# Float64 weight tiles on the sync queue, nine steps ahead in three buffers, and later reciprocal products in the first three pairs of heads

## The chip, the cores and the metric

The kernel runs on one core of a Trainium2 chip. The metric is the device time of one execution in microseconds. Engines are named as in the profile: PE is the matrix engine (PEld its weight loads), DVE the vector engine, ACT the scalar engine, POOL GpSimd, SP the sync engine, which only issues transfers. An engine works through its own instructions in order, and so does the queue that it issues transfers from.

## The reference, cut to what matters

Block-sparse attention over 4 batches of 8 heads (768 rows, head size 64), then a dense two-layer network on the joined heads:

```python
scores = np.where(mask, scale * np.matmul(q, k.transpose(0, 1, 3, 2)), -1e9)
attn = np.exp(scores - scores.max(-1, keepdims=True))
attn = attn / (attn.sum(-1, keepdims=True) + 1e-09)
x = np.matmul(attn, v)                    # joined to [3072, 512]
h = x @ w_in                              # w_in [512, 2048], float64
g = np.where(h >= 1, h, np.where(h <= -1, 0, (h + 1) ** 2 / 4))
out = g @ w_out                           # w_out [2048, 512], float64
```

The two weight matrices arrive as float64. [...]

## The kernel before, in words

**Steps.** All work is put on one plan: `at(t, fn)` gives a piece of work a time in steps, and the list sorted by these times is the order in which the pieces are written down. The framework then arranges each engine's instructions by this order and by its own estimate of when each is ready, so neighbours may change places. One step is one 128-column chunk of scores for half a head (384 rows); a head has 12 steps, head i starts at step 12 i. The constants `P`, `PW` (the first eight heads, called wide) and others hold each piece's distance in steps.

**A head.** `load_qk` (L214) loads q and k, `hi` and `lo` split them, four kinds of moves (L221, L237, L238, on SP) place the parts in KA, QA, KB, QB. `max_mm` (L267, PE) and `max_red` (L272, DVE) find row maxima, which `max_row` (L283) writes into QA. Then per step `scores` (L303, L304, PE), `expo` (L308, ACT) and `values`. For the first five pairs of heads (`WHOLE`) `values` is one full-precision matmul (L333); later heads split the exponentials in two (L196 on ACT, L316 on DVE) and use two (L335, L336), and POOL adds up the sums (L323).

**Reciprocals.** At the end of a pair of heads, for each half `hf`, the denominators go out to DRAM (`r_in`, L377 on ACT's queue), back as a small tile (L378, SP), through `recip` (L372, DVE), out again (`r_out`, L382, SP) and back spread over partitions (L384, SP: den<-s). Then `x_mul` (L387, DVE) multiplies the half's result by them, `x_hi` (ACT) and `x_lo` (L395, DVE) split it into x, which the network reads. These three stand at distances `xm`, `xh`, `xl` from a common time.

**Conversions.** `convert` makes three pieces of work: `load` (L162) brings 128 x 512 float64 values (512 KB) into a tile `raw`; `bits` is one ACT instruction (L168, Abs) and four DVE instructions (L169, L170, L172, L174), of which L172 and L174 read raw again; `split` rounds the high part (L196, ACT) and subtracts for the low one (L180, POOL). Conversion n stands at time t; its load stands at t - P["cl"], its split at t + 1.705. There are 16 of w_in, at CONV + n CSTEP, during the eight heads of batch 0, and 16 of w_out, every 3 steps from step 98.98 on, during the first half of the network. The w_out parts are also stored to DRAM (`w_keep`, L448, SP) right after the split, and later halves load them from there (L441).

**The network.** `moe` runs eight halves (4 batches, 2 halves of 384 rows), the first from step 99.67, each over 16 chunks of the inner dimension, 3 steps a chunk: first layer L457 to L459, nonlinearity L463 to L478, second layer L485 to L487. They run beside the next batch's heads; the last two run after the attention.

**Queues.** Every transfer is issued on SP except the raw tiles (`Q_RAW`, POOL) and `r_in`'s first one (ACT).

Of the kernel before, what the change touches and what calls it, by code (L numbers as in the profile page):

```python
# [10 lines left out]
I32 = mybir.dt.int32  # L11
# [7 lines left out]
B, H, S, D = 4, 8, 768, 64  # L19
# [5 lines left out]
NP = H // 2  # L25
# [3 lines left out]
KA = 96 + T  # L29
# [8 lines left out]
def body(ctx, tc, qk_t, v, sampled_blocks, moe_w_in, moe_w_out, ind, cm, negd, ident, fold, out):  # L38
    nc = tc.nc
    pool = lambda name, bufs, **kw: ctx.enter_context(tc.tile_pool(name=name, bufs=bufs, **kw))  # L40
    cst = pool("cst", 1)
    ld = pool("ld", 1)
# [7 lines left out]
    mt = pool("mt", 2)  # L50
    op = pool("op", 1)
    wst = pool("wst", 3)
    cv = pool("cv", 1)
# [12 lines left out]
    Q_KEEP = nc.sync  # L66
    Q_W = nc.sync
    Q_OUT = nc.sync
    Q_RAW = nc.gpsimd
    Q_QK = nc.sync  # L70
    Q_V = nc.sync

    def f(ap):
        return ap.bitcast(F32)
# [12 lines left out]
    def consts():  # L87
        M = slice(64, KM)
        for i in range(SETS):
            nc.gpsimd.memset(f(QA[i][64:128 if i == 0 else 96]), 0.0)  # L90
        nc.gpsimd.memset(VW[0][:, :, 64:128], 1.0)
        nc.gpsimd.memset(VW[1][:, :, 0:64], 1.0)
        nc.vector.memset(eps, 1e-9)
        nc.vector.memset(half_c, 0.5)
        sraw = cst.tile([128, NR, 2], I32, name="sraw")
        nc.sync.dma_start(out=sraw[M], in_=sampled_blocks.bitcast(I32).rearrange("a (r w) -> a r w", w=2))
        cmt = cst.tile([128, 2 * NB], F32, name="cmt")
        nc.sync.dma_start(out=cmt[M], in_=cm)
        ef = f(cv.tile([128, 512, 2], I32, name="raw", bufs=2).rearrange("p c w -> p (c w)"))[64:KA, 0:S]
        nc.sync.dma_start(out=ef, in_=ind)  # L100
        idf = pp.tile([128, HALF], F32, name="pt")[:, 0:128]
        nc.sync.dma_start(out=idf, in_=ident)
        nc.vector.tensor_copy(out=idr, in_=idf)
        nc.vector.tensor_copy(out=KAt[0][64:KA], in_=ef)
        nc.sync.dma_start(out=nd, in_=negd.rearrange("a (t p) -> a t p", t=T))
        nc.sync.dma_start(out=sel, in_=fold)
        for i in range(1, SETS):
            rounded(nc.gpsimd, KAt[i][64:KA], ef)
        sf = cst.tile([128, NR], F32, name="sf")
        nc.vector.tensor_copy(out=sf[M], in_=sraw[M, :, 0])  # L110
        al = cst.tile([128, NB], F32, name="al")
        nc.vector.tensor_copy(out=al[M], in_=cmt[M, 0:NB])
        for r in range(NR):
            nc.vector.scalar_tensor_tensor(
                out=al[M], in0=cmt[M, NB:2 * NB], scalar=sf[M, r:r + 1], in1=al[M],
                op0=ALU.is_equal, op1=ALU.max)
        mb = cst.tile([128, NB], F32R, name="mb")
        nc.vector.tensor_scalar(out=mb[M], in0=al[M], scalar1=-1.0, scalar2=BIG, op0=ALU.add, op1=ALU.mult)
        for hf in range(2):
            cs = slice(hf * HALF, (hf + 1) * HALF)  # L120
            pm = psa.tile([128, 512], F32, name="pa")
            nc.tensor.matmul(out=pm[0:NB, 0:HALF], lhsT=mb[M], rhs=KAt[0][64:KM, cs], start=True, stop=True)
            for i in range(SETS):
                (nc.scalar.copy if i else nc.vector.tensor_copy)(out=QA[i][64:KM, cs], in_=pm[0:NB, 0:HALF])
# [4 lines left out]
    def at(t, fn, *args):  # L129
        plan.append((t, fn, args))  # L130
# [18 lines left out]
    def plan_conversions():  # L149
        last = 1e9  # L150
        for t, load, bits, split in sorted(conv, key=lambda x: -x[0]):
            last = t = min(t, last - P["cd"])
            at(t - P["cl"], load)
            at(t, bits)
            at(t + P["cs"], split)

    def convert(t, src, dst, done=None):
        st = {}

        def load():  # L160
            st["raw"] = cv.tile([128, 512, 2], I32, name="raw", bufs=2)
            Q_RAW.dma_start(out=st["raw"], in_=src.bitcast(I32).rearrange("p (c w) -> p c w", w=2))  # L162

        def bits():
            raw = st["raw"]
            lo32, hi32 = raw[:, :, 0], raw[:, :, 1]
            a = st["a"] = cv.tile([128, 512], I32, name="cva", bufs=2)
            nc.scalar.activation(out=f(a), in_=f(hi32), func=AF.Abs)  # L168
            nc.vector.tensor_scalar(out=f(a), in0=f(a), scalar1=CLO, scalar2=CHI, op0=ALU.max, op1=ALU.min)  # L169
            nc.vector.tensor_scalar(out=a, in0=a, scalar1=3, scalar2=0x3FFFFFFF,  # L170
                                    op0=ALU.logical_shift_left, op1=ALU.bitwise_and)
            nc.vector.scalar_tensor_tensor(out=a, in0=hi32, scalar=-0x40000000, in1=a,  # L172
                                           op0=ALU.bitwise_and, op1=ALU.bitwise_or)
            nc.vector.scalar_tensor_tensor(out=a, in0=lo32, scalar=29, in1=a,  # L174
                                           op0=ALU.logical_shift_right, op1=ALU.bitwise_or)

        def split():
            hi, lo = dst()
            rounded(CH, hi, f(st["a"]))
            nc.gpsimd.tensor_tensor(out=lo, in0=f(st["a"]), in1=f(hi), op=ALU.subtract)  # L180
            if done:
                done()

        conv.append((t, load, bits, split))
# [13 lines left out]
    def head(i, n0, b, h, pst):  # L198

        j, e = divmod(h, 2)  # L200
        wide = i < H
        whole = i // 2 in WHOLE
        G = {**P, **PW} if wide else {**P, **PA} if i < 2 * H else P
        o0, o1 = (L, R) if e == 0 else (R, L)
        QAi, KAi = QA[i % SETS], KAt[i % SETS]
        st = {}
# [191 lines left out]
        for hf in range(2):  # L398
            for c in range(T):
                at(s, scores, hf, c)  # L400
                at(s + G["ex"], expo, c)
                if not whole:
                    at(s + G["ph"], p_hi, c)
                    at(s + G["pl"], p_lo, c)
                    at(s + G["ps"], p_sum, hf, c)
                at(s + G["lag"], values, hf, c)
                s += 1
            u = s - 1 + G["lag"]
            if whole:
                at(u + G["ow"], o_whole, hf)  # L410
            else:
                at(u + G["ot"], o_tmp)
                at(u + G["oa"], o_add, hf)
                at(u + G["al"], acc_sum, hf)
                if e:
                    at(u + G["su"], sums, hf)
                    at(u + G["de"], dens, hf)
            if e:
                y = u + (G["yw"] if whole else G["yy"])
                if whole:  # L420
                    at(y, r_in, hf)
                    y += G["r1"]
                at(y, recip, hf)
                at(y + 0.1, r_out, hf)
                y -= G["r1"]
                y += G["r2"]
                at(y + G["xm"], x_mul, hf)
                at(y + G["xh"], x_hi, hf)
                at(y + G["xl"], x_lo, hf)
# [4 lines left out]
    def moe(t0, p, b, hf, first):  # L434

        g = {}
        G = {**P, **PM} if first else P

# [4 lines left out]
        def w_dst(fi):  # L443
            w = g["w", fi] = wst.tile([128, 2, DM], F32R, name="w")
            return w[:, 0], w[:, 1]
# [60 lines left out]
        for fi in range(NF):  # L506
            u = t0 + fi * p
            if first:
                convert(u + 1.5 * p - P["co"], moe_w_out[fi * 128:(fi + 1) * 128, :], lambda fi=fi: w_dst(fi),
                        lambda fi=fi: w_keep(fi))  # L510
# [16 lines left out]

    at(TC, consts)
    for i in range(NHEADS):
# [5 lines left out]
    p = PER * H / (2 * NF)  # L535
# [3 lines left out]
    for fq in range(4):  # L539
        for kt in range(4):  # L540
            cs = slice(fq * 512, (fq + 1) * 512)
# [10 lines left out]


WHOLE = (0, 1, 2, 3, 4)
P = {'vw': 4.0, 'r1': 0.857, 'r2': 4.031, 'qs': 9.647, 'ks': 11.666, 'vs': 9.131, 'ld': 5, 'm0': 7.832, 'm1': 5.0, 'mr': 0.46, 'mc': 2.3, 'mt': 1.325, 'mw': 0.9, 'ex': 0.524, 'ph': 1.22, 'pl': 1.349, 'ps': 0.841, 'ow': 0.704, 'ot': 0.2, 'oa': 0.549, 'ah': 0.3, 'al': 0.578, 'su': 0.637, 'de': 1.414, 'yw': 0.799, 'yy': 2.173, 'xm': 0.774, 'xh': 1.0, 'xl': 2.518, 'gr': 0.1, 'gs': 0.279, 'gm': 0.314, 'gh': 0.934, 'gl': 1.232, 'l2': 1.494, 'l3': 0.158, 'l1': 0.121, 'cl': 3.327, 'cs': 1.705, 'cd': 1.8, 'co': 5.196, 'lag': 3.5}
PW = {'vw': 4.0, 'r1': 3.302, 'r2': 4.413, 'qs': 12.454, 'vs': 9.131, 'ld': 5, 'm0': 7.8, 'm1': 5.61, 'mr': 0.15, 'mc': 2.3, 'mt': 1.3, 'mw': 0.9, 'ex': 0.2, 'ph': 1.231, 'pl': 1.349, 'ps': 0.841, 'ow': 0.722, 'ot': 0.2, 'oa': 0.462, 'ah': 0.3, 'al': 0.578, 'su': 0.637, 'de': 1.525, 'yw': 0.813, 'yy': 2.024, 'xm': 0.516, 'xh': 1.1600000000000001, 'xl': 2.268, 'lag': 3.403}
TC = -90
H0 = 0.711
PH1 = ()
PH2 = ()  # L560
# [10 lines left out]
NHEADS = B * H  # L571
NMOE = B
PER = 2 * T
CONV, CSTEP = 6.105, 5.609
CLO, CHI = (struct.unpack("<f", struct.pack("<I", w))[0] for w in (0x38100000, 0x47EFFFFF))

_INS = ["qk_t", "v", "sampled_blocks", "moe_w_in", "moe_w_out"]
# [49 lines left out]
```

## Time and profile before

| | us |
|---|---|
| median of 3 runs (lowest, highest) | 1031.86 (1029.77, 1033.98) |
| profiled execution, its own time | 1029.55 |
| span in the profile | 1027.5 |
| PE busy | 956.7 |
| DVE busy | 751.0 |
| ACT busy | 635.4 |
| POOL busy | 396.0 |

The span runs from the first to the last instruction; the profiled execution's own time is a little more. An engine's busy time is the time in which at least one of its instructions ran. In the views a line such as L162 is a line of the kernel, `raw<-in_moe_w_in_dram` is what it writes and reads, and in a view of waits "A <- B: us, times, longest" says that A stood idle until B was done.

### The profile page before, as it was taken

How to read it: one execution, taken by the hardware profiler on the slowest of the kernel's cores; microseconds unless marked ns; L12 is line 12 of the kernel's file. 1: busy time of each engine (PE TensorE's matmuls, PEld its weight loads, DVE VectorE, ACT ScalarE, POOL GpSimd, SP SyncE). 2: the span in 40 equal slices, each digit the busy share in tenths (PEclk: the TensorE clock that was granted, in tenths of full speed). 3: DMA queues.
4: the chain of work that ended last, by engine and by line, in shares of the span. 5: the costliest groups of instructions: out<-in, count | busy, mean ns of one | idle time of the engine just before them, and what ended most of it. 6: DMA issues, size and time to landing. Idle time of an engine off the chain costs nothing.

```text
span 1027.5 us, 14635 instructions
## 1 busy us (share of the span) xinstructions
PE 956.7 (93%) x4687; PEld 828.1 (81%) x4687; DVE 751.0 (73%) x1317; ACT 635.4 (62%) x1302; POOL 396.0 (39%) x347
## 2 busy tenths in 40 slices
PE   3889887998889999999999999999999999999998
PEld 2556565777778989888988888988988899899997
DVE  5877787768999787888888887888888786422222
ACT  3566565557657666766767676766667666533433
POOL 3424233236656445454545445453545444100000
PEclk9999899999999999999999999999999999999999
DMA  6656666746435555554535455554535452433433
GB/s 169 184 153 168 182 157 199 217 146 187 152 121 165 146 146 152 147 173 127 156 122 162 137 162 152 147 167 125 151 120 178 131 144 83 149 124 123 154 131 105
DMA packets 56216, 154.43 MB, mean 150 GB/s; under 512 B 9612, under 2 KB 17952, under 8 KB 56140
## 3 DMA queue, kind: packets, MB, share of 16 engines
q1 hardware_dynamic: 51492, 136.70, 44.9%
q0 software_dynamic: 4608, 16.78, 5.6%
q8 instruction: 37, 0.61, 0.2%
q14 instruction: 39, 0.32, 0.1%
q10 hardware_dynamic: 40, 0.03, 0.0%
HBM read 100.92 MB, written 14.81 MB: 113 GB/s over the span
## 4 chain that ended last, share of the span: by engine, by line
PE 60%; DVE 12%; ACT 2%; DMA 2%; issue 2%; SPq 0%; ACTq 0%
PE oa L485 7%; PE oa L487 7%; PE oa L486 7%; PE hp L457 6%; PE hp L459 6%; PE hp L458 6%; PE po L335 4%; PE pa L303 4%; PE pa L304 4%; PE po L336 4%; PE pa L267 3%; DVE mc L272 3%; DVE pl L316 3%; DMA qk<-in_qk_t_dram 2%; DVE gl L478 2%; DVE xun L387 2%
## 5 line engine op out<-in xcount | busy, mean ns | idle before, releaser
L323 POOL TENSOR_TENSOR acc<-acc,pt 128x384 f32<-128x384 f32 x176 | 198.3, 1127 | 202.4 <-ACT pt L308 184.5
L272 DVE TENSOR_REDUCE mc<-pa 128x1 f32<-128x384 f32 x384 | 202.8, 547 | 23.7 <-PE pa L267 20.9
L316 DVE TENSOR_TENSOR pl<-pt,ph 128x384 fp32r<-128x384 f32 x264 | 177.5, 672 | 36.7 <-ACT ph L196 35.8
L196 ACT CAST ph<-pt 128x384 fp32r<-128x384 f32 x264 | 135.6, 514 | 98.2 <-PE po L335 94.9
L308 ACT ACTIVATE pt<-pa 128x384 f32<-128x384 f32 x288 | 140.6, 489 | 57.3 <-PE pa L304 48.5
L267 PE MATMUL pa<-KA,QA 88*128 88x384 f32 x384 | 143.4, 390 | 28.1 <-DVE mc L272 18.5
L457 PE MATMUL hp<-x,wi 128*128 128x384 f32 x448 | 156.9, 350 | 5.3 <-DVE r L469 5.3
L485 PE MATMUL oa<-w,gh 128*128 128x512 f32 x384 | 153.6, 400 | 0.3 <-ACT gh L196 0.3
L458 PE MATMUL hp<-x,wi 128*128 128x384 f32 x448 | 152.2, 340 | 0.0
L459 PE MATMUL hp<-x,wi 128*128 128x384 f32 x448 | 151.6, 338 | 0.0
L487 PE MATMUL oa<-w,gl 128*128 128x512 f32 x384 | 151.5, 395 | 0.0
L486 PE MATMUL oa<-w,gh 128*128 128x512 f32 x384 | 150.9, 393 | 0.0
L478 DVE TENSOR_TENSOR gl<-r,gh 128x384 fp32r<-128x384 f32 x128 | 102.6, 802 | 30.6 <-ACT gh L196 28.7
L267 PEld LDWEIGHTS pa<-KA,QA 88*128 88x128 f32 x384 | 73.9, 194 | 59.9 <-DVE mc L272 35.1
L469 DVE SCALAR_TENSOR_TENSOR r<-r,hp 128x384 f32<-128x384 f32 x112 | 61.6, 550 | 74.8 <-ACT r L466 74.8
L228 POOL TENSOR_TENSOR qk<-qk,qkh 128x768 f32<-128x768 f32 x32 | 62.1, 1940 | 119.0 <-ACT qkh L196 110.3
L303 PE MATMUL pa<-QA,KA 102*128 102x384 f32 x288 | 100.8, 350 | 6.2 <-DVE mc L272 5.2
L304 PE MATMUL pa<-QB,KB 128*128 128x384 f32 x288 | 98.1, 341 | 0.0
L463 ACT ACTIVATE r<-hp,half_c 128x384 f32<-128x384 f32 x112 | 65.1, 581 | 52.8 <-PE hp L459 49.7
L335 PE MATMUL po<-ph,vn 128*128 128x384 f32 x264 | 92.0, 349 | 4.2 <-DVE xun L345 3.2
L457 PEld LDWEIGHTS hp<-x,wi 128*128 128x128 f32 x448 | 84.8, 189 | 12.3 <-DVE r L469 7.8
L336 PE MATMUL po<-pl,vn 128*128 128x384 f32 x264 | 88.8, 336 | 0.0
(99 smaller groups left out, 1720.7 us busy)
## 6 DMA issues: line engine op xcount, KB each, us to landing
w<-wo_dram SPq DMA_DIRECT2D x112, 512.0 KB
qk<-in_qk_t_dram SPq DMA_DIRECT2D x32, 384.0 KB
raw<-in_moe_w_in_dram POOLq DMA_DIRECT2D x16, 512.0 KB, 6.2
raw<-in_moe_w_out_dram POOLq DMA_DIRECT2D x16, 512.0 KB, 4.2
wo_dram<-w SPq DMA_DIRECT2D x16, 512.0 KB
lv<-in_v_dram SPq DMA_DIRECT2D x32, 192.0 KB
KA<-qkh SPq DMA_DIRECT2D x32, 192.0 KB
QA<-qkh SPq DMA_DIRECT2D x32, 192.0 KB
```

The source lines that it names most:

```text
L267: nc.tensor.matmul(out=pm[:, 0:HALF], lhsT=QAi[0:KM, t * 128:(t + 1) * 128], rhs=KAi[0:KM, kh * HALF:(kh + 1) * HALF], start=True, stop=True)
L272: nc.vector.reduce_max(out=st["mc"][:, t, kh:kh + 1], in_=st.pop(("pm", t, kh))[:, 0:HALF], axis=AX.X)
L303: nc.tensor.matmul(out=ps[:, 0:HALF], lhsT=KAi[0:KA, ks], rhs=QAi[0:KA, cs], start=True, stop=False)
L308: nc.scalar.activation(out=p, in_=st.pop(("ps", c))[:, 0:HALF], func=AF.Exp, scale=SCALE)
L316: (nc.gpsimd if i < 2 * H and c in PL1 else nc.vector).tensor_tensor(out=pl, in0=st["p", c], in1=f(st["ph", c]), op=ALU.subtract)
L323: nc.gpsimd.tensor_tensor(out=st["acc", hf], in0=prev, in1=st["p", c], op=ALU.add)
L457: nc.tensor.matmul(out=hv, lhsT=wi[:, j, 0, fs], rhs=x[:, 0], start=(j == 0), stop=False)
L458: nc.tensor.matmul(out=hv, lhsT=wi[:, j, 0, fs], rhs=x[:, 1], start=False, stop=False)
L459: nc.tensor.matmul(out=hv, lhsT=wi[:, j, 1, fs], rhs=x[:, 0], start=False, stop=(j == NP - 1))
L485: nc.tensor.matmul(out=o, lhsT=gh[:, ts], rhs=w[:, 0], start=(fi == 0), stop=False)
L486: nc.tensor.matmul(out=o, lhsT=gh[:, ts], rhs=w[:, 1], start=False, stop=False)
L487: nc.tensor.matmul(out=o, lhsT=gl[:, ts], rhs=w[:, 0], start=False, stop=(fi == NF - 1))
```

## The change

The raw tiles are loaded on SP's queue instead of POOL's. Their tile has three buffers instead of two (the constant `ef`, which is read once at the start, uses the same buffers). The load stands 9.0 steps before its conversion instead of 3.327. The w_in conversions stand at 8.0 + 5.75 n instead of 6.105 + 5.609 n; the w_out conversions stay where they were. For the first three pairs of heads, `x_mul`, `x_hi` and `x_lo` stand two steps later; the transfers before them do not move.

```diff
-    Q_RAW = nc.gpsimd
+    Q_RAW = nc.sync
...
-        ef = f(cv.tile([128, 512, 2], I32, name="raw", bufs=2).rearrange("p c w -> p (c w)"))[64:KA, 0:S]
+        ef = f(cv.tile([128, 512, 2], I32, name="raw", bufs=3).rearrange("p c w -> p (c w)"))[64:KA, 0:S]
...
-            st["raw"] = cv.tile([128, 512, 2], I32, name="raw", bufs=2)
+            st["raw"] = cv.tile([128, 512, 2], I32, name="raw", bufs=3)
...
-                y += G["r2"]
+                y += G["r2"] + (XLATE if wide and j < NP - 1 else 0)
...
-P = {..., 'cl': 3.327, ...}
+P = {..., 'cl': 9.0, ...}
...
+XLATE = 2.0
...
-CONV, CSTEP = 6.105, 5.609
+CONV, CSTEP = 8.0, 5.75
```

More of the change, by code (lines that the diff above doesn't have):

```diff
@@ L554 @@
 WHOLE = (0, 1, 2, 3, 4)
-P = {'vw': 4.0, 'r1': 0.857, 'r2': 4.031, 'qs': 9.647, 'ks': 11.666, 'vs': 9.131, 'ld': 5, 'm0': 7.832, 'm1': 5.0, 'mr': 0.46, 'mc': 2.3, 'mt': 1.325, 'mw': 0.9, 'ex': 0.524, 'ph': 1.22, 'pl': 1.349, 'ps': 0.841, 'ow': 0.704, 'ot': 0.2, 'oa': 0.549, 'ah': 0.3, 'al': 0.578, 'su': 0.637, 'de': 1.414, 'yw': 0.799, 'yy': 2.173, 'xm': 0.774, 'xh': 1.0, 'xl': 2.518, 'gr': 0.1, 'gs': 0.279, 'gm': 0.314, 'gh': 0.934, 'gl': 1.232, 'l2': 1.494, 'l3': 0.158, 'l1': 0.121, 'cl': 3.327, 'cs': 1.705, 'cd': 1.8, 'co': 5.196, 'lag': 3.5}
+P = {'vw': 4.0, 'r1': 0.857, 'r2': 4.031, 'qs': 9.647, 'ks': 11.666, 'vs': 9.131, 'ld': 5, 'm0': 7.832, 'm1': 5.0, 'mr': 0.46, 'mc': 2.3, 'mt': 1.325, 'mw': 0.9, 'ex': 0.524, 'ph': 1.22, 'pl': 1.349, 'ps': 0.841, 'ow': 0.704, 'ot': 0.2, 'oa': 0.549, 'ah': 0.3, 'al': 0.578, 'su': 0.637, 'de': 1.414, 'yw': 0.799, 'yy': 2.173, 'xm': 0.774, 'xh': 1.0, 'xl': 2.518, 'gr': 0.1, 'gs': 0.279, 'gm': 0.314, 'gh': 0.934, 'gl': 1.232, 'l2': 1.494, 'l3': 0.158, 'l1': 0.121, 'cl': 9.0, 'cs': 1.705, 'cd': 1.8, 'co': 5.196, 'lag': 3.5}
 PW = {'vw': 4.0, 'r1': 3.302, 'r2': 4.413, 'qs': 12.454, 'vs': 9.131, 'ld': 5, 'm0': 7.8, 'm1': 5.61, 'mr': 0.15, 'mc': 2.3, 'mt': 1.3, 'mw': 0.9, 'ex': 0.2, 'ph': 1.231, 'pl': 1.349, 'ps': 0.841, 'ow': 0.722, 'ot': 0.2, 'oa': 0.462, 'ah': 0.3, 'al': 0.578, 'su': 0.637, 'de': 1.525, 'yw': 0.813, 'yy': 2.024, 'xm': 0.516, 'xh': 1.1600000000000001, 'xl': 2.268, 'lag': 3.403}
 TC = -90
+XLATE = 2.0
 H0 = 0.711
```

## The prediction

> **What bounds the kernel now.** I read the page first, for the engines' shares; then busy time by stretches, cut where the exponentials show a head's beginning; then the waits of each engine inside the stretch that stands out; then the timeline of a few places in it. The page:
>
> ```profile
> span 1027.5 us, 14635 instructions
> PE 956.7 (93%) x4687; PEld 828.1 (81%) x4687; DVE 751.0 (73%) x1317; ACT 635.4 (62%) x1302; POOL 396.0 (39%) x347
> raw<-in_moe_w_in_dram POOLq DMA_DIRECT2D x16, 512.0 KB, 6.2
> ```
>
> and of the view of the raw tiles (ns min/median/max, first and last start):
>
> ```profile
> L162 POOL DMA_DIRECT2D raw<-in_moe_w_out_dram x16: 580/580/594, 136.8 to 287.0; - x16
> L174 DVE SCALAR_TENSOR_TENSOR cva<-raw,cva x32: 616/691/2320, 15.8 to 307.1; 128x512 int32<-128x512 int32 x32
> ```
>
> PE, at 93%, is the bound on average. Three stretches (columns: length, then busy us and count of PE, PEld, DVE, ACT, POOL, then granted clock, DMA share, GB/s): the eight heads of batch 0, which share the time with the sixteen w_in conversions; the next four heads, beside the first MoE half and the w_out conversions; the rest of the attention. The fourth row is one wide pair of heads with its clock, the last a later head.
>
> ```profile
> 24.00:168.00 144.00, 122.26 (x482) 85.78 (x483) 114.13 (x202) 87.16 (x181) 46.32 (x40) 0.98 0.63 170
> 168.00:305.00 137.00, 120.46 (x551) 98.92 (x550) 111.71 (x182) 84.28 (x171) 63.93 (x55) 0.98 0.53 168
> 305.00:880.00 575.00, 562.48 (x2918) 509.30 (x2917) 470.63 (x828) 397.46 (x831) 276.48 (x237) 1.00 0.50 145
> 94.00:132.00 38.00, 33.10 (x126) 23.46 (x126) 29.21 (x52) 22.79 (x48) 12.05 (x11) 0.91 0.62 160
> 334.00:363.00 29.00, 29.00 (x153) 26.27 (x152) 22.54 (x42) 19.80 (x42) 13.83 (x13) 1.00 0.49 139
> ```
>
> After 305 us PE is idle 12.5 us in 575, and the last raw load went out at 287.0: the change can do nothing there but start it earlier. From 24 to 168 us, 96 steps at 1.50 us each (144/96), no engine is full: PE is idle 21.7 us, DVE 29.9, ACT 56.8. From 168 to 305 PE is idle 16.5 us and DVE 25.3. These two stretches are where the change acts. The waits in the first (us in total, times, longest):
>
> ```profile
> ACT cva L168 <- DMA raw<-in_moe_w_in_dram: 24.0, 13, 3.8
> ACT cva L168 <- DMA raw<-in_moe_w_out_dram: 8.6, 3, 4.4
> DVE cva L169 <- ACT cva L168: 8.8, 6, 3.0
> DVE xun L387 <- DMA den<-s: 5.2, 3, 2.0
> DVE mc L272 <- PE pa L267: 8.2, 9, 1.9
> PE pa L267 <- DVE mc L272: 11.0, 8, 2.4
> SPq L214 <- DMA KB<-qk: 35.5, 8, 7.4
> SPq L378 <- DMA s<-den: 17.6, 3, 6.6
> ```
>
> ACT stands 32.6 us (24.0 + 8.6) in front of a raw tile that has not landed, with the exponentials queued behind. DVE then stands 8.8 us for ACT's Abs, and 5.2 us for a denominator still under way; behind both stand the row maxima that PE waits for (11.0 us). The timeline shows why the tile is late:
>
> ```profile
> 78.53 0.58 POOL L162 DMA_DIRECT2D raw<-in_moe_w_in_dram  x1 [0.96 <-DVE cva L170]
> 81.00 0.59 POOL L162 DMA_DIRECT2D raw<-in_moe_w_in_dram  x1
> 88.06 0.66 ACT L168 ACTIVATE cva<-raw 128x512 f32<-128x512 f32 x1 [3.68 <-DMA raw<-in_moe_w_in_dram]
> 89.87 0.67 ACT L168 ACTIVATE cva<-raw 128x512 f32<-128x512 f32 x1 [0.78 <-DMA raw<-in_moe_w_in_dram]
> 97.15 0.58 POOL L162 DMA_DIRECT2D raw<-in_moe_w_in_dram  x1 [0.96 <-DVE cva L174]
> 104.20 0.43 DVE L169 TENSOR_SCALAR cva<-cva 128x512 f32<-128x512 f32 x1 [3.02 <-ACT cva L168]
> 107.05 0.56 DVE L387 TENSOR_TENSOR xun<-xun,den 128x384 f32<-128x384 f32 x1 [1.96 <-DMA den<-s]
> ```
>
> A load goes out only when L174 has freed one of two buffers, lands 7 to 10 us later (81.00 to 89.87), and ACT is at its Abs by then. So the conversions run in a ring: free, load, wait, convert, free. It turns about once in 18.6 us (78.53 to 97.15) for two conversions, while two plan intervals of 5.609 steps are 16.8 us.
>
> **The change part by part.**
>
> *Loads nine steps ahead, three buffers, in the wide stretch.* The lead grows from 3.327 steps (5.0 us) to 9 steps (13.5 us), against a landing of 6.2 us in the median. With conversions 5.75 steps apart, load n needs the buffer that conversion n-3 read 17.25 steps before its own turn, 8.25 steps before the load: the third buffer is free in time. ACT's 32.6 us then go. They are not all worth time: PE's own idle time caps any gain in this stretch at 21.7 us, and the floor is nothing. Between these I take what reached DVE, which is nearer to PE's waits than ACT is: 8.8 us. The price that could turn it round is in SP, below. What is late next is DVE waiting for PE's maxima (8.2 us) and PE for DVE's.
>
> *Products two steps later.* Two steps are 3.0 us; the longest wait of L387 is 2.0. All three waits in the stretch (5.2 us) belong to the moved products, since heads 6 and 7 end after it. x is read only in the first MoE half, and by the plan the next pair writes the two den buffers at steps 9.1 and 15.1 after a pair's end, five steps after the moved products (4.1 and 10.1), so nothing new waits: I take 5.2 us; ends 0, if DVE stops at its next instruction instead, and 11.0, if all of PE's wait for maxima came from it.
>
> *The conversions' places.* The w_in conversions start at step 8.0 instead of 6.1 and end at 94.25 instead of 90.24; the first MoE half starts at 99.67 and needs the last four of them only 36 steps later. The work is the same, so 0; the cover is those 36 steps.
>
> *The clock.* The fourth row's 0.91 means 38 x 0.09 = 3.4 us of lost clock. I take 0 of it, end 3.4.
>
> *w_out stretch.* The waits there:
>
> ```profile
> DVE cva L169 <- ACT cva L168: 11.4, 6, 3.1
> ACT cva L168 <- POOL w L180: 6.6, 7, 1.5
> ACT cva L168 <- DMA raw<-in_moe_w_out_dram: 4.2, 2, 3.5
> POOL raw L162 <- DVE cva L174: 19.4, 7, 9.4
> POOL raw L162 <- ACT w L196: 4.8, 1, 4.8
> POOL raw L162 <- ACT pt L308: 4.7, 1, 4.7
> POOL raw L162 <- ACT r L466: 4.4, 1, 4.4
> POOL raw L162 <- PE po L333: 3.7, 1, 3.7
> SPq L448 <- POOL w L180: 54.1, 11, 9.4
> ```
>
> Here only 4.2 us of ACT's waiting is for raw. POOL stands 37.0 us (five rows) in front of a load, and behind it stands the subtraction L180, for which SP waits 54.1 us with its stores and everything queued after them. Taking the load off POOL frees L180. Against that, nine steps are exactly three conversions of 3 steps, so on SP each load waits for the buffer that L174 of conversion n-3 is just then freeing. Gain at most DVE's 11.4 us; loss at most the 37.0 us, moved to SP. I take a gain of 2.0, about half of the 4.2, because SP waits for L180 of that same conversion right after anyway.
>
> *The queue.* POOL loses 32 issues of 0.58 us, 18.6 us of an engine busy 39%: nothing. SP gains 32 issues:
>
> ```profile
> 88.33 0.33 SPq L214 DMA_DIRECT2D qk<-in_qk_t_dram  x1
> 97.63 0.32 SPq L382 DMA_DIRECT2D s<-rc  x1
> 103.16 1.38 SPq L384 DMA_DIRECT2D den<-s  x2
> ```
>
> at 0.33 us (the input load of L214), 10.6 us in some 290. In the queue they now stand behind SP's waits, the longest 7.4 and 6.6 us: a lead of 13.5 less a landing of 6.2 leaves 7.3, which just covers one such wait and not two. Behind them stand the moves into KA, QA, QB, KB (planned 12 steps ahead, 18 us) and the den round trip (s<-rc at 97.63 to den<-s at 103.16 is one hop of 5.5 us). Cost taken: 0; ends 0 and the rival below.
>
> The Trainium skill, "DMA: Bandwidth & Descriptors", section "Issuing engines are not separate DMA queues", says that issuing from several engines saves only the sequencer's issue time. By that the change of queue alone is worth nothing and the sum would be 14.0 instead of 16.0; POOL's 37.0 us of waiting in its own queue speaks for somewhat more.
>
> *The start.*
>
> ```profile
> 12.37 0.66 ACT L168 ACTIVATE cva<-raw 128x512 f32<-128x512 f32 x1 [7.59 <-DMA raw<-in_moe_w_in_dram]
> 13.07 0.43 DVE L169 TENSOR_SCALAR cva<-cva 128x512 f32<-128x512 f32 x1 [3.56 <-ACT cva L168]
> 14.36 1.42 PE L267 MATMUL pa<-KA,QA 88*128 88x384 f32 x3 [4.75 <-DMA QA<-qkh]
> ```
>
> The first conversion held DVE 3.56 us ahead of the mask copy, but QA's move ended PE's wait at the same moment. A third buffer lets a second 512 KB go out early, on the queue of that move: 512 KB at the stretch's 170 GB/s is 3.1 us by estimate. Ends +3.1 and -3.6; taken 0.
>
> Sum: 8.8 + 5.2 + 2.0 = 16.0 us. The profiled execution took 1029.55 us (span 1027.5 and 2.05 around it), so 1013.5; the median of the runs shown stands 2.3 above it, so 1015.9, rounded to 1016. As a check, the wide stretch would fall to 130 us, with PE busy 94% of it, below the 98% after 305 us.
>
> **The rivals.**
>
> *The next wait takes the place.* DVE and ACT are in order and tied to PE; DVE's L174 takes 0.6 to 2.3 us, and without the pauses the same work may just meet more of it. For it: DVE <- PE already stands at 8.2 us. Against: the three busiest engines all have idle time that begins with a late transfer. Then only a third of the sum stays, 5 us: 1027.
>
> *Slower: SP held by the raw loads in the w_out stretch.* Sixteen loads inherit POOL's 37.0 us of waiting, and behind them now stand the moves of the next head and the den round trips rather than sums. If all of it reached PE, the time would be 1031.9 + 37.0 - 14.0 = 1055; from 19 us on (14.0 and the 5.2 of 0.5%) it is slower by what can be told. Against: SP stands before L180 of the same conversions already. The Trainium skill, "DMA: Bandwidth & Descriptors", section "Queues, rings and completion order", has each DMA engine take a ring in order and go round between queues; so a move behind a raw tile on SP's ring would wait for it, where POOL's queue shared. No run here shows it.
>
> *More than the sum.* All of PE's idle time and lost clock in the wide stretch goes: 21.7 + 3.4 + 2.0 = 27.1, so 1005. Against: PE stays idle 2% even where nothing is loaded.
>
> **How the numbers follow.** The forecast has 0.60, the next wait 0.20, SP held 0.10, more than the sum 0.10. A measurement here tells about 0.5%, 5.2 us. Faster by more: 0.60 and 0.10, and 0.05 of the next wait's case, 0.75; within: 0.15, the rest of that case and a little of the forecast's low end; slower 0.10. The range reaches from 1003, the third rival with a little to spare, to 1030, which takes in the next wait; the forecast's own is 1008 to 1024.
>
> **What would show it.** Right: ACT's wait for raw between 24 us and the ninth head falls from 32.6 us to under 5; L387's 5.2 us go; the ninth head begins near 154 us instead of 168; the stretch of four heads after it stays near 135 us; from the thirteenth head on nothing differs. Wrong: the raw waits gone and the ninth head still at 163 or later (next wait); the four heads longer than 150 us with SP waiting at the load line for L174 (SP held); the raw waits still there, because the loads stand behind SP's own.

## The result, and the profile after

The changed kernel takes 1017.07 us (median of four, 1016.05 to 1022.08) against 1031.68 us for the kernel before: a ratio of 0.987, 95% interval [0.984, 0.989]. A second set gave 1019.18 us and 0.987 [0.984, 0.990]. The forecast was 1016. The time came out as predicted. The reasons did not, as the experiments show. (The execution of the kernel before that was profiled took 1029.55 us at a granted clock of 0.993 over its span, a good one: the others of that kernel, 61 beside the experiments, had 0.979 to 0.990. One more, of 1544 us, was in a slower state of the chip and is left out.)

The profiled execution of the changed kernel took 1022.08 us, 5 above the median. The head of its page, and then its busy time by stretches (columns as in the prediction: length, busy us and count of PE, PEld, DVE, ACT, POOL, granted clock, DMA share, GB/s). The stretches are divided as before at the first exponential of the first, ninth and thirteenth heads, rounded.

```profile
span 1020.3 us, 14628 instructions
PE 960.8 (94%) x4687; PEld 831.5 (81%) x4687; DVE 748.1 (73%) x1317; ACT 636.7 (62%) x1302; POOL 376.1 (37%) x315
```

```profile
18.00:165.00 147.00, 129.78 (x500) 92.67 (x500) 127.64 (x220) 94.52 (x190) 41.62 (x27) 0.97 0.67 189
165.00:293.00 128.00, 117.33 (x542) 95.87 (x541) 102.98 (x171) 80.49 (x164) 53.25 (x40) 0.99 0.51 162
```

A second profile of the same kernel, of an execution of 1015.21 us, has the same shape:

```profile
18.00:161.00 143.00, 126.53 (x501) 90.24 (x501) 126.06 (x220) 94.56 (x191) 41.52 (x27) 0.99 0.69 195
161.00:291.00 130.00, 119.63 (x541) 97.77 (x539) 102.10 (x171) 80.17 (x163) 52.87 (x40) 0.96 0.50 159
```

In what follows the wide stretch is the eight heads of batch 0, from the first exponential of the first head to that of the ninth; the start is what lies ahead of it; the four heads are the ninth to the twelfth. Against before: the first head's exponentials begin at 17.7 us instead of 23.6, six earlier. The wide stretch is no shorter, 143.4 and 147.4 us against 144.5, where 130 was forecast. The four heads after it take 128.1 and 130.4 us against 136.5, where no change was forecast. The rest is within a few us. So the gain lies at the start and in the w_out stretch, the two places that the prediction had put at 0 and 2.0.

The waits in the wide stretch after, per engine (us in total, times, longest):

```profile
DVE cva L169 <- ACT cva L168: 7.1, 7, 1.9
DVE mc L272 <- PE pa L267: 6.6, 11, 1.3
...
PE pa L267 <- DVE mc L272: 5.5, 5, 1.9
PE oa L303 <- DVE QA L283: 5.1, 5, 1.3
PE pa L280 <- DVE mr L276: 2.2, 2, 1.9
...
ACT cva L168 <- DMA raw<-in_moe_w_in_dram: 0.9, 1, 0.9
...
SPq L162 <- DVE cva L174: 13.1, 5, 6.5
```

and of before, PE's other two waits for DVE:

```profile
PE oa L303 <- DVE QA L283: 1.4, 2, 1.1
...
PE pa L280 <- DVE mr L276: 0.8, 2, 0.5
```

ACT's 32.6 us in front of raw tiles are down to 0.9, and L387's 5.2 are gone; PE's wait for the reductions to row maxima (L272) halved, from 11.0 to 5.5. But PE's waits for the next steps of the same chain on DVE grew, for L276 from 0.8 to 2.2 and for L283 from 1.4 to 5.1: together PE waits 12.8 us for DVE, against 13.2 before. The late transfers were removed as promised, and the stretch did not shorten. The view of the raw tiles (duration in ns, then first and last start) shows what came in its place, and with it DVE's group of L174 in the wide stretch, first of before, then of the changed kernel (count, then busy us, mean ns, idle time before it):

```profile
L162 SPq DMA_DIRECT2D raw<-in_moe_w_in_dram x16: 328/380/534, 12.5 to 104.5; - x16
L162 SPq DMA_DIRECT2D raw<-in_moe_w_out_dram x16: 328/374/539, 111.5 to 262.6; - x16
```

```profile
L174 DVE SCALAR_TENSOR_TENSOR cva<-raw,cva 128x512 int32<-128x512 int32 x16 | 18.5, 1159 | 0.3
```

```profile
L174 DVE SCALAR_TENSOR_TENSOR cva<-raw,cva 128x512 int32<-128x512 int32 x21 | 19.5, 929 | 0.5
```

The first w_out tile is requested at 111.5 us, 25 us earlier than before (136.8). L174, which ends a conversion's work on the raw tile, has run 21 times when the ninth head begins, against 17 before (the 16 shown and one ahead of the stretch): four more conversions were drawn forward (five of w_out instead of one), and DVE is busy 126 to 128 us in the stretch, up from 114. The four DVE instructions of the conversions make up that difference: 65.6 us against 51.8.

### The profile page after: what moved, and what is told of

Its sections match the earlier page's. It is cut to its first block, busy times and chain, and to the rows that moved or that the text cites. A ratio compares the mean times of both kernels' runs of the same rounds, so it can differ in the third digit from the quotient of the medians.

```text
span 1020.3 us, 14628 instructions
## 1 busy us (share of the span) xinstructions
PE 960.8 (94%) x4687; PEld 831.5 (81%) x4687; DVE 748.1 (73%) x1317; ACT 636.7 (62%) x1302; POOL 376.1 (37%) x315
## 4 chain that ended last, share of the span: by engine, by line
PE 63%; DVE 18%; DMA 8%; ACT 4%; issue 4%; POOL 1%; SPq 1%; ACTq 0%; POOLq 0%; DVEq 0%
PE oa L485 7%; PE oa L487 6%; PE oa L486 6%; PE hp L457 6%; PE hp L459 5%; PE hp L458 5%; PE pa L267 4%; DVE mc L272 4%; PE po L335 4%; PE pa L303 3%; PE pa L304 3%; PE po L336 3%; DVE pl L316 3%; DMA qk<-in_qk_t_dram 3%; PE oa L333 2%
## 5 line engine op out<-in xcount | busy, mean ns | idle before, releaser
L272 DVE TENSOR_REDUCE mc<-pa 128x1 f32<-128x384 f32 x384 | 203.3, 548 | 32.2 <-PE pa L267 29.7
L308 ACT ACTIVATE pt<-pa 128x384 f32<-128x384 f32 x288 | 140.2, 488 | 55.2 <-PE pa L304 47.3
L267 PE MATMUL pa<-KA,QA 88*128 88x384 f32 x384 | 142.8, 390 | 17.6 <-DVE mc L272 12.0
L228 POOL TENSOR_TENSOR qk<-qk,qkh 128x768 f32<-128x768 f32 x32 | 61.2, 1913 | 124.7 <-ACT qkh L196 95.0
```

Source lines behind the costliest of these rows:

```text
L267: nc.tensor.matmul(out=pm[:, 0:HALF], lhsT=QAi[0:KM, t * 128:(t + 1) * 128], rhs=KAi[0:KM, kh * HALF:(kh + 1) * HALF], start=True, stop=True)
L272: nc.vector.reduce_max(out=st["mc"][:, t, kh:kh + 1], in_=st.pop(("pm", t, kh))[:, 0:HALF], axis=AX.X)
L308: nc.scalar.activation(out=p, in_=st.pop(("ps", c))[:, 0:HALF], func=AF.Exp, scale=SCALE)
```

## The experiments

All were run in five rounds with the kernel before on the same chip; each ratio is to that kernel, with its 95% interval. Its medians there were 1030.6 to 1031.9 us.

| label | kernel | median us | ratio |
|---|---|---|---|
| again | changed kernel | 1019.18 | 0.987 [0.984, 0.990] |
| after_noxlate | changed, products not moved | 1019.01 | 0.987 [0.985, 0.990] |
| before_xlate | before, products two steps later | 1032.47 | 1.001 [0.999, 1.003] |
| after_pool | changed, raw tiles on POOL | 1034.23 | 1.003 [1.001, 1.005] |
| before_sync | before, raw tiles on SP | 1007.76 | 0.977 [0.975, 0.979] |
| before_firstsync | before, first raw tile on SP | 1034.24 | 1.002 [1.000, 1.005] |
| after_hold | changed, w_out's Abs held to the ninth head | 1014.91 | 0.983 [0.981, 0.985] |
| after_cva4 | changed, four buffers of cva | 1017.92 | 0.987 [0.984, 0.989] |
| after_oldplaces | changed, old conversion places | 1024.41 | 0.993 [0.990, 0.996] |
| after_late | changed, two buffers, lead 3.327 | 1009.38 | 0.978 [0.975, 0.980] |
| before_pool4 | before, four buffers, no load stands for one | 1021.99 | 0.991 [0.988, 0.994] |
| after_bufs2 | changed, two buffers | 1004.72 | 0.976 [0.973, 0.979] |

### Is it repeatable, and are the products worth anything?

*again*: the changed kernel as it is.

> The changed kernel once more, for a second profile: the first one was of an execution of 1022.1 us, 5 above the median. Theory P (the prediction's: raw waits and den waits of the wide stretch give 14 us): the ninth head begins near 154 us and the wide stretch is near 130 us long. Theory S (the start gives 6 us, since the first raw load no longer stands before the mask copy, and the rest comes from conversions whose DVE work moves forward out of the four heads after, the wide stretch itself staying near 144): first exponential near 18 us, ninth head at 161 to 166, the four heads after it 128 us or less. Both: 1015 to 1018 us.

*after_noxlate* undoes the later products, *before_xlate* makes them alone.

```diff
 # after_noxlate
-XLATE = 2.0
+XLATE = 0.0
 # before_xlate (XLATE = 2.0)
-                y += G["r2"]
+                y += G["r2"] + (XLATE if wide and j < NP - 1 else 0)
```

> The changed kernel with the products of the first three pairs where they were. P: the waits of L387 come back, some 5 us of DVE in the wide stretch, and 5.2 us of time: 1022. S: the products are off the path, within 2 us of the changed kernel: 1015 to 1019.

> The kernel before with the products of the first three pairs two steps later, and nothing else. P: 5.2 us faster, 1026.5. S: no difference that can be told, 1029 to 1034.

*again* came out near theory S in its marks (first exponential at 17.6 us, ninth head at 161.0), with four heads of 130.4 us instead of 128 or less and a time just above the 1015 to 1018 of both theories. The products moved nothing: 1019.01 beside 1019.18, and 1032.47 beside 1031.94. DVE's group in the wide stretch of after_noxlate, with the idle time before it last, and then DVE's wait in that of before_xlate:

```profile
L387 DVE TENSOR_TENSOR xun<-xun,den 128x384 f32<-128x384 f32 x6 | 3.3, 548 | 0.0
```

```profile
DVE xun L387 <- DMA den<-s: 6.8, 3, 3.2
```

Without the later products nothing waits for den, once the raw tiles are on SP; with them, but the raw tiles on POOL, L387 waits 6.8 us (5.2 before). In these kernels the wait goes with the queue of the raw tiles, not with the products' place.

### Queue, or lead and buffers?

*after_pool* keeps everything but the queue; *before_sync* changes the queue alone.

```diff
 # after_pool
-    Q_RAW = nc.sync
+    Q_RAW = nc.gpsimd
 # before_sync
-    Q_RAW = nc.gpsimd
+    Q_RAW = nc.sync
```

> The changed kernel with the raw loads on POOL's queue again (three buffers and nine steps kept). P: the queue is worth about 2 us, 1018 to 1019. S: the first loads go out near 3 us again beside the first moves, the first exponential is at 22 us or later and 4 to 7 us are lost: 1021 to 1024.

> The kernel before with all raw loads on SP's queue, two buffers, 3.327 steps ahead, old places: the queue alone. S: the start's 6 us and nothing else, 1025 to 1027, about 17 conversions done at the ninth head. Theory Q (what counts besides the start is that POOL no longer waits for raw buffers ahead of its subtractions in the four heads after): first exponential at 18, four heads 130 us instead of 137, 1018 to 1020. P: 1030, since raw waits stay.

The queue is all of the gain and more. Both times lie outside what any of the theories had expected, the first above and the second below. Lead, buffers, places and products without it give 1034.23, a little slower than before. The queue without them gives 1007.76, 23 us faster than before and some 10 faster than the full change. The stretches of before_sync:

```profile
17.00:155.00 138.00, 126.25 (x507) 90.78 (x505) 118.43 (x210) 91.65 (x187) 38.22 (x26) 0.99 0.65 185
155.00:281.00 126.00, 116.20 (x536) 96.78 (x535) 102.24 (x180) 82.57 (x168) 56.65 (x42) 0.97 0.55 176
```

The start is 6.2 us shorter than before, the wide stretch 7.4, the four heads 9.7 (17.4, 137.1, 126.8 us by the exponentials' own times). Its waits in the wide stretch:

```profile
SPq L162 <- DVE cva L174: 15.9, 5, 5.2
...
DVE cva L169 <- ACT cva L168: 7.5, 5, 2.3
...
ACT cva L168 <- DMA raw<-in_moe_w_in_dram: 0.3, 1, 0.3
```

With two buffers and the old lead ACT no longer waits for a raw tile; the standing for a buffer is now SP's. In after_pool the raw waits fell as well, yet its wide stretch stayed at 144.5 us. Its waits there, and its row of the stretches:

```profile
DVE xun L387 <- DMA den<-s: 10.3, 3, 3.9
...
ACT cva L168 <- DMA raw<-in_moe_w_in_dram: 6.8, 4, 2.8
...
POOL raw L162 <- DVE cva L174: 10.6, 7, 1.9
POOL raw L162 <- DVE cva L169: 9.9, 1, 9.9
...
POOL raw L162 <- ACT wi L196: 2.9, 1, 2.9
POOL raw L162 <- DVE cva L170: 1.9, 2, 1.0
```

```profile
30.00:174.00 144.00, 127.98 (x488) 92.58 (x487) 114.80 (x202) 90.52 (x184) 48.83 (x43) 0.93 0.66 183
```

Here DVE waits 10.3 us for den, though the products stand two steps later, and the granted clock is 0.93, 10 us of the stretch lost by that (144 x 0.07). POOL now stands 25.3 us (four rows) in front of raw loads, against 9.7 in this stretch before:

```profile
POOL raw L162 <- DVE cva L174: 7.8, 6, 1.7
POOL raw L162 <- DVE cva L170: 1.9, 2, 1.0
```

Taking ACT's raw waits away was thus not enough: DVE waits elsewhere, POOL stands longer, and PE runs slower. Whether den is late because the raw tiles travel on the other queue at the same time fits these rows and before_sync's, but was not isolated.

### The start

The transfer timelines of before and of the changed kernel show the first raw tile, and then the copy of the block mask into QA on DVE (L124), which the first head needs:

```profile
2.93 0.69 POOL L162 DMA_DIRECT2D raw<-in_moe_w_in_dram  x1
...
13.52 1.01 DVE L124 CAST QA<-pa 24x384 fp32r<-24x384 f32 x2
```

```profile
8.96 1.01 DVE L124 CAST QA<-pa 24x384 fp32r<-24x384 f32 x2
11.58 2.92 PE L267 MATMUL pa<-KA,QA 88*128 88x384 f32 x6 [2.54 <-DMA QA<-qkh]
12.53 0.46 SPq L162 DMA_DIRECT2D raw<-in_moe_w_in_dram  x1
```

On POOL the tile goes out at 2.93 us, before the moves into QA have run; on SP it stands behind them and goes out at 12.53. The moves land earlier (the first max matmul stands for QA until 11.58 instead of 14.36), and DVE reaches its mask copy before the first conversion, not after it. *after_pool* confirms the direction: it sends two tiles early and starts its exponentials at 29.7 us.

```profile
2.93 1.23 POOL L162 DMA_DIRECT2D raw<-in_moe_w_in_dram  x2
...
16.01 1.50 PE L267 MATMUL pa<-KA,QA 88*128 88x384 f32 x3 [7.31 <-DMA QA<-qkh]
```

*before_firstsync* moves that one load alone.

```diff
-            Q_RAW.dma_start(out=st["raw"], ...)
+            (nc.sync if t == CONV else Q_RAW).dma_start(out=st["raw"], ...)
```

> The kernel before with only the first of the 32 raw loads on SP's queue, where it stands behind the first head's moves; all else as before. Theory S (the start is worth 6 us): the mask copy no longer waits behind the first conversion, first exponential at 18 us instead of 24, 1025 to 1027 us. Theory P (start worth nothing, raw waits of the wide stretch 9 us): 1031 to 1033.

The start fell to 17.8 us, but the kernel took 1034.24, no less than before: the wide stretch took 150.0 us and the four heads 144.2.

```profile
18.00:168.00 150.00, 131.66 (x491) 96.02 (x490) 115.21 (x205) 89.78 (x183) 46.11 (x41) 0.91 0.60 162
168.00:312.00 144.00, 123.75 (x548) 102.87 (x547) 113.59 (x186) 84.38 (x171) 65.55 (x57) 0.93 0.53 168
```

The granted clock is 0.91 and 0.93, 13.5 and 10.1 us lost (150 x 0.09, 144 x 0.07), against 2.9 and 2.7 before (0.98 in both, 144 and 137 us). The six us exist, and with the other tiles still on POOL they are given back. The time missed both theories, S by 7 us and P by one. The fall of the clock is not a matter of the one profile: over whole executions it was 0.977 to 0.983 in the twelve of this kernel (0.980 on average) and 0.981 to 0.988 in the seventeen of the kernel before beside them (0.985), which is 5 us of 1034 by estimate. Why it falls is not shown.

### What the third buffer does

If early w_out conversions cost time, holding them back should help (*after_hold*), and if the two buffers of `cva`, the tile that a conversion works in, were the limit, more of them should (*after_cva4*).

```diff
 # after_hold (mark[0]: the ninth head's first exponential; done: the w_out conversions)
-            nc.scalar.activation(out=f(a), in_=f(hi32), func=AF.Abs)
+            with tc.issue_after(mark[0]) if done else ExitStack():
+                nc.scalar.activation(out=f(a), in_=f(hi32), func=AF.Abs)
 # after_cva4
-            a = st["a"] = cv.tile([128, 512], I32, name="cva", bufs=2)
+            a = st["a"] = cv.tile([128, 512], I32, name="cva", bufs=4)
```

> The changed kernel with the w_out conversions held: no Abs of one before the first exponential of the ninth head on ACT, so 16 conversions are done there and not 21. If the wide stretch is bound by what DVE and ACT do in it, it shrinks from about 144 to 134 or 136 us and the four heads after it grow to 137: 1016 to 1020 in all. If the wide stretch is bound by something else, it stays near 144, the four heads grow by 2 us for each of five conversions, and the time is 1025 to 1028.

> The changed kernel with four buffers for the converted bits instead of two: 23 or 24 conversions can stand before the tenth head instead of 21. If the conversions moved forward into the wide stretch are what shortens the four heads after (about 2 us each), those heads take 124 us and the time is 1011 to 1014. If not (Q), no difference: 1015 to 1019.

after_hold's stretches, and its group of L174 (L176 there) in the first:

```profile
17.00:158.00 141.00, 125.55 (x495) 89.96 (x494) 114.09 (x202) 89.98 (x181) 37.99 (x25) 0.98 0.63 178
158.00:289.00 131.00, 120.02 (x550) 100.14 (x548) 115.73 (x191) 84.77 (x173) 57.13 (x43) 0.96 0.57 181
```

```profile
L176 DVE SCALAR_TENSOR_TENSOR cva<-raw,cva 128x512 int32<-128x512 int32 x16 | 12.9, 803 | 0.4
```

It gains about 4 us (1014.91 beside 1019.18; 0.983 [0.981, 0.985] beside 0.987 [0.984, 0.990], which just overlap). Its wide stretch, with 16 conversions, is 140.2 us, still 3 above before_sync's, and its four heads take 131.5. after_cva4 changes nothing. I had held that the four heads are 2 us shorter for each conversion moved out of them; that fell, since after_hold moved five back and was not slower.

*after_oldplaces* has CONV, CSTEP = 6.105, 5.609; *after_late* has two buffers and the old lead; *after_bufs2* has two buffers and keeps the nine steps. (The line of `ef` changes along with the tile.)

```diff
 # after_late and after_bufs2
-            st["raw"] = cv.tile([128, 512, 2], I32, name="raw", bufs=3)
+            st["raw"] = cv.tile([128, 512, 2], I32, name="raw", bufs=2)
 # after_late only
-P = {..., 'cl': 9.0, ...}
+P = {..., 'cl': 3.327, ...}
```

> The changed kernel with the w_in conversions at their old places (from step 6.105, every 5.609); queue, three buffers, nine steps stay. L: 1015 to 1018. M: 1007 to 1010.

> The changed kernel with two raw buffers and the load 3.327 steps ahead again; queue, later products and new places of the w_in conversions stay. Theory L (nine steps and a third buffer draw conversions forward into the wide stretch and cost the 9 us by which the queue alone is better than the whole change): 1007 to 1010. Theory M (the new places cost it): 1016 to 1019.

> The changed kernel with two raw buffers, all else kept, the nine steps too. If it is the third buffer that lets conversions move forward into the wide stretch and costs 8 us, the wide stretch is 137 us with 18 conversions done at its end, and the time 1007 to 1011. If it is the nine steps of lead, the stretch stays at 143 to 147 and the time at 1015 to 1019.

The old places cost 5 us (1024.41 beside 1019.18), which neither theory had expected. With two buffers the places are worth nothing that can be told: after_late, with the new ones, is at 0.978 and before_sync, with the old ones, at 0.977. Two buffers instead of three, and nothing else, give 1004.72: the third buffer costs 12 us by the ratios ((0.987 - 0.976) x 1031 with more digits; 14 by the medians, taken on different chips), and the two intervals, [0.984, 0.990] and [0.973, 0.979], lie apart. That is more than the theory of the third buffer had said (1007 to 1011). The lead of nine steps does no harm: 1004.72 with it, 1009.38 without, and those intervals overlap. The stretches of after_bufs2, DVE's group in the first, and its w_in loads:

```profile
17.00:154.00 137.00, 124.63 (x500) 89.62 (x500) 117.91 (x209) 91.55 (x186) 37.53 (x25) 0.99 0.66 185
154.00:279.00 125.00, 115.11 (x525) 94.19 (x525) 105.70 (x176) 80.39 (x163) 56.92 (x41) 0.97 0.56 178
```

```profile
L174 DVE SCALAR_TENSOR_TENSOR cva<-raw,cva 128x512 int32<-128x512 int32 x18 | 16.4, 910 | 0.3
```

```profile
L162 SPq DMA_DIRECT2D raw<-in_moe_w_in_dram x16: 327/416/537, 12.1 to 128.6; - x16
```

In the wide stretch DVE has 18 conversions instead of 21 and is 8 to 10 us less busy, and the stretch is 6 to 10 us shorter. The four heads, which must do the conversions left over, are not longer: 127.5 us. That fits the reading that conversions drawn forward cost time where DVE is busiest and buy none back. But after_hold returned five conversions and recovered only 4 us, so their order is a part of it; the other 8 to 10 us of the third buffer stay open. The length of the wide stretch goes with the time that PE waits for DVE in it, added up over the rows of PE's waits: 16.1 us in before_firstsync (150.0 us long), 12.8 and 12.0 in the changed kernel (147.4 and 143.4), 11.3 in after_hold (140.2), 8.4 in after_bufs2 (137.3), 8.3 in before_sync (137.1), 5.3 in before_pool4 of the next section (134.4); 15.9 in after_pool (144.5) is out of line. This is a pattern over single profiles, not a test. Two buffers hold the loads back by themselves: the nine-step load cannot leave until L174 of two conversions earlier, as the last w_in request at 128.6 us shows (104.5 with three).

### Why is POOL's queue dear?

One answer is that the loads stand for a buffer in POOL's order, with subtractions behind them. *before_pool4* stays on POOL, with four buffers, and writes each load behind a POOL subtraction after which its buffer is free, so that no load stands for one.

```diff
-name="raw", bufs=2
+name="raw", bufs=4
...
+            with tc.issue_after((first + subs)[max(0, len(loads) - 2)]):
                 Q_RAW.dma_start(out=st["raw"], ...)
```

(`first` is the first head's POOL subtraction L228, `subs` the conversions' L180.)

> The kernel before, its raw loads still on POOL, but with four buffers and each load put in POOL's order behind a subtraction after which its buffer is long free (the first three behind the first head's subtraction, load n behind that of conversion n-3). POOL no longer waits for a raw buffer and the loads are early. Theory B (what the queue change took away is POOL's standing in its own order and ACT's wait for late tiles): 1007 to 1013. Theory R (a load from POOL's queue itself costs, by its slower landing or by what writing its descriptors does to the other engines): 1022 or more.

Its stretches, and its waits (L173, L185 and L456 are L168, L180 and L448 there): ACT's for raw tiles in the first stretch and in the second, then POOL's and SP's in the second:

```profile
20.00:154.00 134.00, 123.07 (x486) 87.60 (x485) 116.68 (x207) 88.69 (x182) 49.38 (x42) 0.97 0.68 187
154.00:295.00 141.00, 124.36 (x556) 102.02 (x555) 110.28 (x185) 84.16 (x170) 63.35 (x54) 0.95 0.55 162
```

```profile
ACT cva L173 <- DMA raw<-in_moe_w_in_dram: 12.9, 6, 5.3
...
ACT cva L173 <- DMA raw<-in_moe_w_out_dram: 4.2, 2, 3.0
...
ACT cva L173 <- DMA raw<-in_moe_w_out_dram: 9.1, 4, 3.9
...
POOL w L185 <- issue: 20.7, 4, 7.1
...
SPq L456 <- POOL w L185: 49.4, 10, 10.2
```

and of before_sync, in its four heads:

```profile
SPq L448 <- POOL w L180: 30.2, 11, 5.5
```

It takes 1021.99 us, between the two theories and at the edge of R: 9 of the 23 us that SP's queue is worth. The start is 19.7 us and the wide stretch 134.4, even shorter than on SP, with 17.1 us of raw waits left (12.9 of w_in, 4.2 of w_out) and none of POOL's standing; the four heads are 140.7, some 14 longer than on SP. after_pool had it the other way round, few raw waits (8.1, of which 1.3 of w_out) and much standing (25.3), and gained nothing. So in the wide stretch it is mostly a load's standing for its buffer in POOL's order that costs, as far as two kernels that differ in more than this can show it.

In the w_out stretch something else of POOL's queue costs, and it was not found. ACT's 9.1 us of raw waits are too few for 14. Two rows say where to look: SP, with its stores, still waits 49.4 us for POOL's subtraction (54.1 before, 30.2 in before_sync), and POOL stands 20.7 us ahead of subtractions for nothing that the profile shows.

The granted clock has a share in all of this that no run separates. Over whole executions it was 0.979 to 0.990 in the kernel before (0.985 in the middle), 0.983 to 0.990 in before_pool4, 0.986 to 0.992 in the changed kernel, 0.993 to 0.997 in after_bufs2 and 0.994 to 1.000 in before_sync. If all of it told on the time, it would be 12 us of the 23 by estimate (1031 x 0.012), and 5 us of the third buffer's 12 to 14. It need not: the profiled execution of the kernel before, at 0.993, took only 2 us less than the median. Whether PE's shorter waits raise the clock, or the clock shortens the time by itself, was not tested.

## Why the prediction was right or wrong, step by step

- **Time.** 1017 for 1016, by terms that cancelled: the queue was worth 23 us and not 2, the third buffer cost 12 to 14 us instead of helping to bring 8.8, the new places of the w_in conversions brought 5 where none was counted, the products brought 0 instead of 5.2. That the sum still came to 16 is luck.
- **Loads nine steps ahead, three buffers: 8.8 taken.** The wait went as said (32.6 to 0.9 us, the mark was 5); the gain did not follow. after_pool has this step without the queue and no gain; after_bufs2 has the queue without the third buffer and is faster. The step that failed here is that what reached DVE, 8.8 us, would come back as time: the wait of L169 for Abs, from which the 8.8 was taken, is still 7.1 us, and PE waits as long for DVE as before. "The third buffer is free in time" was read as harmless: the loads moved up so far that SP stands 13.1 us at the load line for L174 all the same, and w_out's conversions could start early, five of them before the ninth head instead of one. "The work is the same, so 0" for the conversions' places missed that a place decides how much work comes before the ninth head; with three buffers the new places are worth 5 us.
- **The products: 5.2 taken, 0 found**, both ways. The waits for den went with the queue. The end 0 of the range was the right one, for another reason than given.
- **The queue: 0 taken, 23 found** (before_sync). This is the step that failed most. I priced the issues (18.6 us on POOL, 10.6 on SP) and feared SP's waits, and counted of POOL's standing only about half of the 4.2 us that showed as ACT's raw wait in the w_out stretch. What it is worth lies in all three places: 6 at the start, 7 in the wide stretch, 10 in the four heads. The 130 us forecast for the wide stretch was nearest in before_pool4 (134.4).
- **A page's rule.** By the Trainium skill, "DMA: Bandwidth & Descriptors", section "Issuing engines are not separate DMA queues", issuing from several engines saves only the sequencer's issue time. The prediction made of it that the change of queue alone is worth nothing; before_sync, at 0.977 [0.975, 0.979] for the queue alone, contradicts that use of it here.
- **The start: 0 taken, -6 found**, beyond the end of -3.6. I looked at what ended PE's wait and not at what stood in front of the move: the transfer of QA came after a raw tile sent at 2.93 us, and without that tile it lands some 3 us earlier, ahead of a mask copy that no conversion delays.
- **The rivals.** "SP held" did not come: SP stands in front of raw loads in before_sync's wide stretch (15.9 us) and the stretch is shorter than before. "The next wait takes the place" describes what the wide stretch did, if the next wait is read as DVE's own added work; but then the time would have been 1027, and what the queue brought elsewhere hid it. Its mark, the raw waits gone and the ninth head at 163 or later, was met by one profile (165.1) and not by the other (161.0).
- **Marks.** The ninth head began at 161 and 165 us, not 154; the four heads took 128 to 130, not 135. The first of these shows that the 14 us of the wide stretch were not found there; "from the thirteenth head on nothing differs" held within 4 us.

## What to carry to other kernels

A transfer's place in the order of its issuing engine is part of its cost: price what stands behind it and what it is sent ahead of, not the issue time. More buffers do not only remove waits; they let later work start sooner, on an engine that may be the busy one, so count the instructions per stretch before and after. Change one part at a time: here the single line that was priced at nothing was worth more than the whole, and the version with one buffer less, at 1004.7 us, beats both kernels. Look at the granted clock of every execution before putting a difference down to waits.

## What the runs showed of the hardware that I had not expected

- The same 512 KB loads, two buffers and lead on POOL's queue left ACT waiting 32.6 us in the wide stretch, on SP's queue 0.3. A part of this is faster landing: from the start of the issue to the end of the last packet, by the packet records of the two traces, a w_in load took 5.4 us in the median on POOL's queue (first packet after 2.0) and 4.3 on SP's (first packet after 1.3). Those 1.1 us are less than the mean wait of 1.8 us before (24.0 in 13).
- The Trainium skill, "DMA: Bandwidth & Descriptors", section "SWDGE vs HWDGE vs iDMA", says that the rings of transfers issued by GpSimd lie in SBUF state that GpSimd writes, and that DVE locks GpSimd out of it in one of its modes. No run here separates this from the rest of the 14 us left open.
- A gain of 6 us at the start could be lost to the granted clock of the following stretches (0.91 and 0.93 against 0.98 and 0.98) although no instruction was added. In the clock records of the two traces each fall is to one half, for 3.4 or 6.8 us: 13.7 us of it in these stretches before, 47.8 in before_firstsync.
